# Decoding the later weights with a byte pass on ScalarE, with a longer cost table and other ranks in the planner

## The chip, the cores and the metric

The kernel runs on one core of one Trainium2 chip. The metric is the device time of one execution in microseconds. TensorE (PE) multiplies, VectorE (DVE), ScalarE (ACT) and GpSimd (POOL) do the elementwise work, and SyncE (SP) issues every DMA. Each of these engines executes its own instruction list in order.

## The reference

Four batches of attention (8 heads, 768 positions, head size 64) are followed by a mixing network. All inputs are 64-bit floats on the host; the weights reach the chip as their raw 64-bit words.

```python
scores = q @ k.T / 8 - slope[h] * dist          # only n_global = 8 first and n_local = 96 last keys kept
a = softmax(scores)                             # with + 1e-9 in the sum
x = a @ v                                       # 4 x 768 x 512
h = relu(x^T @ w_tok1) @ w_tok2                 # token mixing, 768 -> 256 -> 768
u = x + h^T
out = u + relu(u @ w_ch1) @ w_ch2               # channel mixing, 512 -> 1536 -> 512
```

## The kernel before, in words

**The work.** Attention is cut into 48 units (12 for each batch; one unit is two heads by 256 queries). A unit is a row of steps: `q` scales the queries, `S` forms scores on PE in two PSUM banks, `max` and `exp` and `norm` make the softmax on DVE, ACT and POOL, `T` and `back` transpose it (the first 20 units on PE, the later ones by DMA as `split`, `turn`, `join`), `V` multiplies by the values on PE into one PSUM bank, and `put` copies that bank out on ACT (`put` then frees it). After a batch's attention comes its token mixing (steps `N`, `J`, `U`, with `ua`, `uh`, `ul` that leave u as a high and a low part), and after it the channel mixing: 24 steps k for each batch (two halves of the positions, m = 0 and 1, by 12 slices f of the hidden layer). Step k has `F` (12 matmuls of 128x384 into one PSUM bank, tile `hp`), `fh` on ACT, `fl` on DVE (frees the bank), and `G` (12 matmuls in two halves of six, tile `acc`, four banks held through the 12 slices). All products are made of three matmuls on high and low parts.

**The weights.** They come as 30 pieces of 128x512 64-bit words: pieces 0 to 5 for the token mixing, then pairs (6 + 2f for `F`, 7 + 2f for `G`) for the 12 slices. `weights(n)` at line 281 decodes a piece into a 32-bit float: `down` (ACT) scales the upper word as a float by 2^-112 into a tile `t`, which has three buffers; `shift` (DVE) moves that left by 3; `upper` (DVE) puts in the sign bit of the upper word; `lower` (DVE) puts in the top three bits of the lower word. Then `high` (ACT) rounds to the high part and `low` (DVE or POOL, whichever the planner takes) subtracts it to get the low part, which frees `t`.

**The order.** No queue is filled in program order. Each step is registered with `add(name, engine, cost, run, after, rank, take, give)`; `Plan.record` (line 110) then plays a list schedule in which an engine that is free takes, of its ready steps whose buffers and banks are to be had, the one with the lowest rank, holds it for the cost in the table and passes on with a fixed latency. A change of the PE's kind of matmul counts 20 in rank. The order so found is written out as the order of every engine's instructions. So a cost or a rank changes the order of all engines from the moment at which the planner first decides otherwise, and the chip waits wherever its times differ from the table's.

The table holds for a piece: `down` 0.6, `shift` 0.45, `upper` 0.75, `lower` 0.85, `high` 0.52, `low` 0.64 on DVE or 1.35 on POOL. `rank` (line 736) gives weights 40 + 12n for the first six and 100 + 12n for the rest, the attention units of batch 1 120 + 8.5i, and the channel steps of batch 0 150 + 5k.

Of the kernel before, what the change touches and what calls it, by code (L numbers as in the profile page):

```python
# [9 lines left out]
F32R = mybir.dt.float32r  # L10
I32 = mybir.dt.int32
U16 = mybir.dt.uint16
I64 = mybir.dt.int64
BF16 = mybir.dt.bfloat16
AF = mybir.ActivationFunctionType
ALU = mybir.AluOpType
# [22 lines left out]
PIECES = 6 + 2 * NF  # L39

DOWN = 2.0 ** -112

HI_MIN = 2.0 ** -15


def f32(ap):
    return ap.bitcast(F32)
# [40 lines left out]
class Plan:  # L88
# [13 lines left out]
    def add(self, name, engine, cost, run, after=(), rank=0.0, take=(), give=(), form=None):  # L102

        costs = engine if isinstance(engine, dict) else {engine: cost}
        self.work[name] = dict(name=name, costs=costs, run=run, after=sorted(set(after)), rank=rank, take=take, give=give,
                               form=form, choice=isinstance(engine, dict))
# [98 lines left out]
class Fast:  # L207
# [73 lines left out]
    def weights(self, n):  # L281

        add, dve, act = self.plan.add, self.dve, self.act
        g = {}

        def load():  # L290
            x, i = self.pieces[n]
            g["w"] = self.wt.tile([P, 512], I64, tag="w", name="w64")
            self.sp.dma_start(out=g["w"], in_=x[:, i:i + 512])

        def words():
            wi = g["w"].bitcast(I32).rearrange("p (n two) -> p n two", two=2)
            return wi[:, :, 0], wi[:, :, 1]

        def down():
            g["t"] = self.io.tile([P, 512], I32, tag="io", name="t32")  # L300
            act.activation(out=f32(g["t"]), in_=f32(words()[1]), func=AF.Copy, scale=DOWN)

        def shift():
            dve.tensor_scalar(out=g["t"], in0=g["t"], scalar1=3, scalar2=None, op0=ALU.logical_shift_left)

        def upper():
            dve.scalar_tensor_tensor(out=g["t"], in0=words()[1], scalar=-0x80000000, in1=g["t"], op0=ALU.bitwise_and,
                                     op1=ALU.bitwise_or)

        def lower():  # L310
            dve.scalar_tensor_tensor(out=g["t"], in0=words()[0], scalar=29, in1=g["t"], op0=ALU.logical_shift_right,
                                     op1=ALU.bitwise_or)

        def high():
            if n < 6:
                dst, i = (self.W1, self.W2)[n // 3], 512 * (n % 3)
                g["h"], g["l"] = dst[0][:, i:i + 512], dst[1][:, i:i + 512]
            else:
                t = self.wt.tile([P, 1024], F32R, tag="w", name="wc")
                g["h"], g["l"] = t[:, :512], t[:, 512:]  # L320
                (self.A, self.Z)[n % 2][n // 2 - 3] = g["h"], g["l"]
            act.copy(out=g["h"], in_=f32(g["t"]))

        def low(engine):
            engine.tensor_tensor(out=g["l"], in0=f32(g["t"]), in1=f32(g["h"]), op=ALU.subtract)

        r = rank("weights", n)
        add(f"w{n}", "sp", 1.85, load, [f"w{n - 1}"] if n else [], rank("load weights", n), ["w", "raw"])
        add(f"down{n}", "act", 0.6, down, [f"w{n}"], r, ["t"])
        add(f"shift{n}", "dve", 0.45, shift, [f"down{n}"], r)  # L330
        add(f"upper{n}", "dve", 0.75, upper, [f"shift{n}"], r)
        add(f"lower{n}", "dve", 0.85, lower, [f"upper{n}"], r, (), ["w", "raw"])
        add(f"high{n}", "act", 0.52, high, [f"lower{n}"], r - 20, ["w"] if n >= 6 else [])
        add(f"low{n}", dict(dve=0.64, pool=1.35), 0, low, [f"high{n}"], r - 20, (), ["t"])


    def load(self, v):
# [26 lines left out]
    def pair(self, v):  # L364
# [70 lines left out]
        def halves(e, back):  # L435

            w, z = 512 - 128 * c0, 128 * c0
            by_pairs = (g["r"] if back else g["p"])[e][:, z:].bitcast(U16).rearrange("p (x two) -> p two x", two=2)
            apart = (g["p"] if back else g["r"])[e].bitcast(U16)[:, :2 * w].rearrange("p (two x) -> p two x", two=2)
            return by_pairs, apart  # L440
# [7 lines left out]
        def turned(e):  # L448
            w = 2 * (512 - 128 * c0)
            self.sp.dma_start_transpose(out=g["p"][e].bitcast(U16)[:, :w].rearrange("p (t r) -> p t r", r=P),  # L450
                                        in_=g["r"][e].bitcast(U16)[:, :w])

# [64 lines left out]
    def tokens(self, b):  # L517
# [14 lines left out]
        def split(m, c):  # L532

            g["r", m, c] = r = self.mix.tile([P, 512], F32, tag="p", name="xr").bitcast(U16)[:, :2 * HC]
            dve.tensor_copy(out=r.rearrange("p (s two x) -> p two s x", s=3, two=2),
                            in_=self.x[b, c, m].bitcast(U16).rearrange("p (s x two) -> p two s x", s=3, two=2))

# [198 lines left out]
def rank(kind, *at):  # L736

    if kind == "weights":
        return 40.0 + 12.0 * at[0] if at[0] < 6 else 100 + 12 * at[0]
    if kind == "load weights":  # L740
        n = at[0]
        return 8 + 3 * n if n < 8 else 30 + 4 * n
    if kind == "load":
        return 2.5 * at[0]
    if kind == "pair":
        v = at[0]
        b, i = divmod(v, PER)
        if b == 0:
            return 10.0 * v
        if b == 1:  # L750
            return 120 + 8.5 * i
        return BATCH * b - 60 + 8.5 * i
    if kind == "mix":
        b, k = at
        if b == 0:
            return -20.0 + k
        return (220 + 2 * k if b == 1 else BATCH * b + 10 + 3 * k)
    if kind == "channel":
        b, k = divmod(at[0], 2 * NF)
        return 150 + 5.0 * k if b == 0 else BATCH * b + 100 + 5.5 * k  # L760


BATCH = 140.0


@with_exitstack
# [5 lines left out]
def dense(ctx, tc, qT, kT, vn, nb, w1, w2, wc1, wc2, out):  # L772
# [98 lines left out]
    def decode(t, src):  # L871
        w = wk.tile([P, 768], I64, tag="dw64", name="dw64")
        n = src.shape[-1]
        nc.sync.dma_start(out=w[:, :n], in_=src)
        wi = w.bitcast(I32).rearrange("p (n two) -> p n two", two=2)[:, :n]
        lo, hi = wi[:, :, 0], wi[:, :, 1]
        ti = t.bitcast(I32)
        nc.vector.tensor_scalar(out=ti, in0=hi, scalar1=1, scalar2=1, op0=ALU.logical_shift_left,
                                op1=ALU.logical_shift_right)
        nc.vector.tensor_scalar(out=t, in0=t, scalar1=HI_MIN, scalar2=None, op0=ALU.max)  # L880
        nc.vector.tensor_scalar(out=ti, in0=ti, scalar1=3, scalar2=0x3FFFFFF8, op0=ALU.logical_shift_left,
                                op1=ALU.bitwise_and)
        nc.vector.scalar_tensor_tensor(out=ti, in0=hi, scalar=-0x40000000, in1=ti, op0=ALU.bitwise_and,
                                       op1=ALU.bitwise_or)
        nc.vector.scalar_tensor_tensor(out=ti, in0=lo, scalar=29, in1=ti, op0=ALU.logical_shift_right,
                                       op1=ALU.bitwise_or)
# [116 lines left out]
```

## Time and profile before

| | |
|---|---|
| median of 3 runs | 625.16 us (624.26 to 625.78) |
| the profiled execution | 626.12 us |
| its span, first to last instruction | 624.3 us |
| mean granted TensorE clock | 0.992 |
| PE busy | 605.2 us, 97% of the span |
| DVE busy | 369.5 us, 59% |
| ACT busy | 258.3 us, 41% |
| POOL busy | 206.2 us, 33% |

Busy times are of the one profiled execution. Matmuls are pipelined: the 12 matmuls of an `F` pass in 2.08 us while the profile gives each about 0.34 us, so PE's pace is read from starts. PEclk is the share of the full clock granted to TensorE: 1.00 is 2.4 GHz and 0.50 is 1.2 GHz. In a tile's name `wc` is a decoded weight, `w` its raw words, `sp` the bank of scores, `op` that of a unit's output, `x` the unit's output in SBUF, `o` a result on its way out.

### The profile page before, as it was taken

The numbers are of one execution on the slowest core, as the hardware profiler recorded it, in microseconds if no ns is written. First come the engines' busy times: TensorE is split into PE (matmuls) and PEld (weight loads), VectorE is DVE, ScalarE is ACT, GpSimd is POOL, SyncE is SP. The second block draws the span as 40 slices with busy tenths as digits, with TensorE's granted clock in tenths as the row PEclk, the third lists the DMA queues.
The fourth block names the chain that finished last, engine by engine and source line by source line (L and its number), as shares of the span: only waits on it lengthen the run. The fifth ranks groups of instructions, "written<-read, shape, count | busy, mean of one in ns | idle before, by whom it ended". The sixth has DMA issues, their size and how long they took to land. (4 is left out here: it accounts for less than half of the span.)

```text
span 624.3 us, 10468 instructions
## 1 busy us (share of the span) xinstructions
PE 605.2 (97%) x3730; PEld 548.0 (88%) x3730; DVE 369.5 (59%) x949; ACT 258.3 (41%) x711; POOL 206.2 (33%) x314
## 2 busy tenths in 40 slices
PE   5899998999999999999899999999999999999996
PEld 3577896998989999889788999898988999999996
DVE  4999999898733315767686437666755455113112
ACT  5899855753532102655543214444334132110110
POOL 4897755563500101534153024444131115000000
PEclk9999997999999999999999999999999999999999
DMA  7960565242550001477785101578742401001001
GB/s 258 395 225 2 203 239 200 91 148 58 120 110 1 2 0 51 64 184 156 165 163 129 38 1 51 126 145 170 168 80 47 61 1 50 1 1 52 0 1 56
DMA packets 84028, 62.63 MB, mean 100 GB/s; under 512 B 69760, under 2 KB 73984, under 8 KB 83968
## 3 DMA queue, kind: packets, MB, share of 16 engines
q1 hardware_dynamic: 83968, 61.88, 37.7%
q8 instruction: 31, 0.51, 0.3%
q14 instruction: 29, 0.24, 0.1%
HBM read 38.80 MB, written 6.29 MB: 72 GB/s over the span
## 5 line engine op out<-in xcount | busy, mean ns | idle before, releaser
L198 PE MATMUL hp<-uh,wc 128*128 128x384 f32 x768 | 211.5, 337 | 0.2 <-DVE wc L198 0.2
L198 PE MATMUL acc<-hh,wc 128*128 128x384 f32 x768 | 200.6, 342 | 0.0
L198 PEld LDWEIGHTS acc<-hh,wc 128*128 128x128 f32 x768 | 138.4, 190 | 9.3 <-issue 7.2
L198 PEld LDWEIGHTS hp<-uh,wc 128*128 128x128 f32 x768 | 140.7, 189 | 2.7 <-issue 0.9
L198 ACT ACTIVATE hh<-hp 128x384 fp32r<-128x384 f32 x96 | 47.1, 490 | 223.9 <-PE hp L198 203.5
L198 DVE SCALAR_TENSOR_TENSOR hl<-hp,hh 128x384 fp32r<-128x384 f32 x96 | 53.1, 553 | 138.6 <-ACT hh L198 138.3
L198 PE MATMUL acc<-hl,wc 128*128 128x384 f32 x384 | 129.7, 338 | 0.2 <-DVE hl L198 0.2
L198 PE MATMUL hp<-ul,wc 128*128 128x384 f32 x384 | 128.8, 336 | 0.0
L198 POOL TENSOR_SCALAR p<-p,st 128x256 f32<-128x256 f32 (+1 forms) x132 | 85.3, 663 | 58.9 <-DVE st L198 16.1
L198 DVE COPY r<-p 128x1024 uint16<-128x1024 uint16 (+1 forms) x95 | 68.9, 735 | 35.8 <-DMA p<-r 19.5
L198 ACT ACTIVATE p<-p,st 128x256 f32<-128x256 f32 (+1 forms) x132 | 63.7, 485 | 30.0 <-DVE st L198 23.1
L198 PEld LDWEIGHTS acc<-hl,wc 128*128 128x128 f32 x384 | 72.8, 190 | 0.5 <-DVE hl L198 0.5
L198 PEld LDWEIGHTS hp<-ul,wc 128*128 128x128 f32 x384 | 72.5, 189 | 0.0
L198 POOL TENSOR_TENSOR ul<-x,uh 128x384 fp32r<-128x384 f32 x24 | 24.9, 1038 | 133.3 <-ACT uh L198 85.4
L198 DVE SCALAR_TENSOR_TENSOR t<-w,t 128x512 int32<-128x512 int32 x60 | 51.8, 864 | 1.1
L198 POOL TENSOR_SCALAR qs<-e,sc 128x256 f32<-128x256 f32 x36 | 21.0, 585 | 91.4 <-DMA e<-pk 58.8
L198 PE MATMUL sp<-e,qs 64*128 64x256 f32 (+1 forms) x304 | 42.8, 397 | 5.7 <-DVE o L198 1.9
L198 PEld LDWEIGHTS sp<-e,qs 64*128 64x128 f32 x304 | 26.6, 196 | 15.9 <-issue 6.7
L198 POOL TENSOR_SCALAR pp<-pp,st 128x256 f32<-128x256 f32 (+1 forms) x60 | 34.8, 597 | 8.0 <-DVE st L198 5.7
L198 POOL TENSOR_TENSOR wc<-t,wc 128x512 fp32r<-128x512 f32 x16 | 22.6, 1415 | 19.9 <-ACT wc L198 18.6
L198 ACT ACTIVATE pp<-pp,st 128x256 f32<-128x256 f32 (+1 forms) x60 | 28.5, 485 | 1.3 <-DVE st L198 1.3
L198 PE MATMUL op<-r,e 128*64 128x128 f32 (+1 forms) x304 | 28.9, 321 | 0.0
(94 smaller groups left out, 736.6 us busy)
## 6 DMA issues: line engine op xcount, KB each, us to landing
w<-wc SPq DMA_DIRECT2D x24, 512.0 KB, 5.3
e<-pk SPq DMA_DIRECT2D x24, 512.0 KB, 3.8
out<-o SPq DMA_DIRECT2D x32, 192.0 KB, 1.9
e<-pk SPq DMA_DIRECT2D x13, 384.0 KB, 3.6
unit<-pk SPq DMA_DIRECT2D x8, 512.0 KB, 8.5
w<-w SPq DMA_DIRECT2D x6, 512.0 KB, 9.1
p<-r SPq DMA_TRANSPOSE x56, 3.2
unit<-pk SPq DMA_DIRECT2D x2, 384.0 KB, 3.8
```

The source lines that it names most:

```text
L198: ins = getattr(self.engine, name)(*args, **kw)
```

## The change

For pieces 12 to 29 the `shift` pass on DVE goes. A new ACT pass, `last`, reads byte 3 of each lower word (stride 8 bytes), scales it by 1/32 with a bias that rounds down, and writes the three bits as an integer into the lower word itself. `ends` (DVE) joins them with the sign bit in the upper word, in place; `whole` (DVE, registered under the old name `lower`) shifts `t` left by 3 and joins it with that word. Pieces 0 to 11 are decoded as before. In the table, for pieces from 6 on, `upper` or `ends` cost 0.85 in place of 0.75, `lower` or `whole` 1.3 in place of 0.85, and `low` on POOL 1.45 in place of 1.35. The ranks of the weights from piece 6 become 100 + 10n, of batch 1's units 140 + 8.5i, and of batch 0's channel steps 140 + 5k.

```diff
+U8 = mybir.dt.uint8
+BYTES = 12
+        def last():
+            w = g["w"].bitcast(U8).rearrange("p (n b) -> p n b", b=8)
+            act.activation(out=words()[0], in_=w[:, :, 3], func=AF.Copy, scale=2.0 ** -5, bias=-15.5 / 32)
+
+        def ends():
+            dve.scalar_tensor_tensor(out=words()[1], in0=words()[1], scalar=-0x80000000, in1=words()[0],
+                                     op0=ALU.bitwise_and, op1=ALU.bitwise_or)
+
+        def whole():
+            dve.scalar_tensor_tensor(out=g["t"], in0=g["t"], scalar=3, in1=words()[1], op0=ALU.logical_shift_left,
+                                     op1=ALU.bitwise_or)
...
         add(f"down{n}", "act", 0.6, down, [f"w{n}"], r, ["t"])
-        add(f"shift{n}", "dve", 0.45, shift, [f"down{n}"], r)
-        add(f"upper{n}", "dve", 0.75, upper, [f"shift{n}"], r)
-        add(f"lower{n}", "dve", 0.85, lower, [f"upper{n}"], r, (), ["w", "raw"])
+        if n >= BYTES:
+            add(f"last{n}", "act", 0.6, last, [f"w{n}"], r)
+            add(f"ends{n}", "dve", UPPER, ends, [f"last{n}", f"down{n}"], r)
+            add(f"lower{n}", "dve", LOWER, whole, [f"ends{n}"], r, (), ["w", "raw"])
+        else:
+            add(f"shift{n}", "dve", 0.45, shift, [f"down{n}"], r)
+            add(f"upper{n}", "dve", 0.75 if n < 6 else UPPER, upper, [f"shift{n}"], r)
+            add(f"lower{n}", "dve", 0.85 if n < 6 else LOWER, lower, [f"upper{n}"], r, (), ["w", "raw"])
         add(f"high{n}", "act", 0.52, high, [f"lower{n}"], r - 20, ["w"] if n >= 6 else [])
-        add(f"low{n}", dict(dve=0.64, pool=1.35), 0, low, [f"high{n}"], r - 20, (), ["t"])
+        add(f"low{n}", dict(dve=0.64, pool=1.35) if n < 6 else LOW, 0, low, [f"high{n}"], r - 20, (), ["t"])
...
-        return 40.0 + 12.0 * at[0] if at[0] < 6 else 100 + 12 * at[0]
+        return 40.0 + 12.0 * at[0] if at[0] < 6 else 100 + 10 * at[0]
...
-            return 120 + 8.5 * i
+            return 140 + 8.5 * i
...
-        return 150 + 5.0 * k if b == 0 else BATCH * b + 100 + 5.5 * k
+        return 140 + 5.0 * k if b == 0 else BATCH * b + 100 + 5.5 * k
...
+UPPER, LOWER, LOW = 0.85, 1.3, dict(dve=0.64, pool=1.45)
```

## Rows read from the trace of the kernel before

**Rows 1.** Busy by stretch: us; PE, PEld, DVE, ACT, POOL (x instructions); PEclk, DMA share, GB/s.
```profile
46.00:79.49 33.49, 33.08 (x243) 26.33 (x241) 32.89 (x100) 29.35 (x91) 26.34 (x42) 1.00 0.26 95
97.00:109.60 12.60, 10.03 (x47) 7.90 (x46) 11.72 (x30) 6.95 (x21) 7.69 (x8) 0.73 0.59 209
109.60:306.00 196.40, 196.23 (x1221) 179.61 (x1221) 118.65 (x302) 84.36 (x224) 59.70 (x85) 1.00 0.37 87
306.00:314.20 8.20, 6.31 (x33) 5.24 (x30) 5.25 (x13) 2.30 (x10) 3.15 (x6) 0.79 0.65 186
314.20:617.80 303.60, 303.40 (x1822) 286.23 (x1821) 145.33 (x339) 89.14 (x229) 67.73 (x93) 1.00 0.31 64
104.00:106.00 2.00, 2.00 (x6) 1.44 (x5) 2.00 (x12) 1.73 (x5) 1.61 (x2) 0.50 0.98 334
87.00:144.00 57.00, 54.20 (x326) 49.15 (x325) 53.05 (x109) 36.36 (x89) 32.83 (x33) 0.94 0.46 165
```

**Rows 2.** PE in order of time, 98 to 110 us: start, us, operation [idle before].
```profile
98.19 1.13 PE L198 MATMUL sp<-e,qs 64*128 64x256 f32 x8
100.40 0.67 PE L198 MATMUL sp<-e,qs 64*128 64x256 f32 x2 [1.08 <-issue]
102.56 2.07 PE L198 MATMUL sp<-e,qs 64*128 64x256 f32 x6 [1.49 <-ACT x L198]
109.83 0.52 PE L198 MATMUL acc<-hh,wc 128*128 128x384 f32 x2
```

**Rows 3.** The chain that ended last, undisturbed steps: start, us, operation.
```profile
461.94 2.30 PE hp L198 x12
465.28 2.08 PE hp L198 x12
469.44 1.06 PE sp L198 x8
```

**Rows 4.** DVE, ACT and POOL in order of time, 99 to 105 us.
```profile
99.75 0.55 DVE L198 SCALAR_TENSOR_TENSOR hl<-hp,hh 128x384 fp32r<-128x384 f32 x1
101.56 0.63 ACT L198 CAST wc<-t 128x512 fp32r<-128x512 f32 x1
101.88 2.36 DVE L198 SCALAR_TENSOR_TENSOR t<-w,t 128x512 int32<-128x512 int32 x2
102.06 0.44 ACT L198 COPY x<-op 128x128 f32<-128x128 f32 x2
102.33 1.36 POOL L198 TENSOR_TENSOR wc<-t,wc 128x512 fp32r<-128x512 f32 x1 [1.37 <-ACT wc L198]
```

**Rows 5.** PE and DVE in order of time, 305 to 315 us.
```profile
305.72 1.09 PE L198 MATMUL op<-r,e 128*64 128x256 f32 x12
307.69 0.56 DVE L198 TENSOR_TENSOR o<-acc,uh 128x384 f32<-128x384 f32 x1 [4.25 <-DMA out<-o]
308.35 0.67 PE L198 MATMUL sp<-e,qs 64*128 64x256 f32 x2 [1.54 <-DVE o L198]
314.15 0.33 PE L198 MATMUL hp<-uh,wc 128*128 128x384 f32 x1
```

**Rows 6.** DVE in order of time: the shift of piece 12; two later passes.
```profile
87.67 0.42 DVE L198 TENSOR_SCALAR t<-t 128x512 int32<-128x512 int32 x1
131.37 1.42 DVE L198 SCALAR_TENSOR_TENSOR t<-w,t 128x512 int32<-128x512 int32 x2
```

**Rows 7.** Groups of instructions by form: busy us, mean ns of one, idle before.
```profile
L198 DVE TENSOR_SCALAR t<-t 128x512 int32<-128x512 int32 x30 | 16.4, 546 | 0.0
L198 ACT ACTIVATE t<-w 128x512 f32<-128x512 f32 x30 | 20.5, 683 | 12.9 <-POOL wc L198 10.2 <-DVE wc L198 2.7
```

**Rows 8.** PE in order of time: batch 1's first and fifth scores, batch 0's first channel step.
```profile
46.14 1.01 PE L198 MATMUL sp<-e,qs 64*128 64x128 f32 x8
70.00 1.13 PE L198 MATMUL sp<-e,qs 64*128 64x256 f32 x8
79.49 0.33 PE L198 MATMUL hp<-uh,wc 128*128 128x384 f32 x1
```

## The prediction
> **What bounds the kernel now.** I read the busy times by engine first, then by stretch, then TensorE's timeline where a stretch was not full, then the other engines at those places, and the groups by form for the prices. The reader is to see in [rows 1] that PE is the bound nearly everywhere. From 109.6 to 306 us it is busy 196.23 of 196.40 us, from 314.2 to 617.8 us 303.40 of 303.60, at a granted clock of 1.00. The changed passes lie between 87 and 144 us, and most of that stretch already has PE full; a faster VectorE is worth nothing there. VectorE is nearly full as well (53.05 of 57 us), and that matters only where PE waits for it.
>
> PE's work is fixed: the change adds and takes away no matmul. So the time can only move by what PE loses in waits, in changes between kinds of matmul, and in time at the lower clock. Two places hold nearly all of the loss after 46 us.
>
> The first is at 99 to 110 us [rows 2]. The first `S` there has passed at 98.19 + 1.06 = 99.25 us (1.06 is an undisturbed `S`, [rows 3]). Up to 109.83 us, 10.58 us, PE does one more `S`, half a `G` and one `F`, which undisturbed take 1.06, 1.04 and 2.08 us, and one change of kind at 0.2 (2.30 against 2.08 in [rows 3]): 4.38 us. The loss is 6.2 us: 1.08 and 1.49 us of idle, and the rest at half clock. The granted clock is 0.50 in 104 to 106 us [rows 1], the 1.2 GHz level, after these waits, with PE working throughout; over 97 to 109.6 us it is 0.73.
>
> Why PE waited there is in [rows 4]. The second `S` needs two banks. One is freed by `fl` on DVE, which ends at 100.30 us; the matmuls begin at 100.40. The other is freed by a `put` on ACT, which begins at 102.06 and stood in ACT's order behind two rounds of decoding. ACT's `high` at 101.56 had waited for DVE's `lower`; the `put` did not need it. A round lasts some 2.75 us (the `lower` before that `high` ended about 101.5, the next ends at 101.88 + 2.36 = 104.24). The table of before gives a round's three DVE passes 0.45 + 0.75 + 0.85 = 2.05 us. So the planner believed that the `put` stood 1.4 us earlier after two rounds than it did, and the error adds up over pieces.
>
> The second place is at 306 to 314 us [rows 5]: PE finished a `V` at about 306.74 and reaches the next `F` at 314.15, 7.41 us for work of 1.06 + 0.2 + 2.08 = 3.34. The loss is 4.1 us, part of it again clock (0.79 over the stretch, [rows 1]). Here VectorE waited 4.25 us for a store to give a tile back, and the bank went late to an `S`.
>
> **The change part by part.** Removed: 18 `shift` passes, pieces 12 to 29, from 87.67 us on [rows 6]. At the group's mean of 0.546 us [rows 7] that is 9.8 us of DVE; the one in [rows 6] took 0.42, so 7.6 us is the lower end. On the path it is worth 0 by itself, since PE is full after 109.6 us and its wait before that is priced below as a place.
>
> `ends` in place of `upper`, `whole` in place of `lower`: the same form of instruction with the same count of elements, and no row shows them with all words 8 bytes apart. Free passes took 1.42 / 2 = 0.71 us [rows 6]; a blocked one 2.36 - 0.71 = 1.65 [rows 4]. I take 0.71 for `ends`, as for `upper`, and no change for `whole`. The far end is 18 x (1.65 - 0.71) = 17 us more of DVE, which would outweigh the shift; it falls in the rival on decoding below.
>
> Added: 18 `last` passes on ACT. No row shows a byte as input; `down` has the same 512 elements and stride and takes 0.683 us [rows 7], so 12.3 us; bounds 0.63 (the cast in [rows 4]) and twice 0.683. ACT is busy 36.36 of 57 us between 87 and 144 us [rows 1] and would be at 48.7: not full. `last` needs only the loaded words, so it need not wait for DVE; but if a `last` is put ahead of a late `put` or `fh`, it delays it by up to 0.68 us. PE's slack covers that after 109.6 us; I take 0. Without that cover, the bound is 12.3 us. SP's and POOL's lists get no new instruction; loads are only released earlier or later by `lower`.
>
> The table: a round is now 0.85 + 1.3 = 2.15 us planned for pieces 12 on, where I expect 0.71 + 0.71 to 1.65, and 2.6 for 6 to 11, where about 2.75 is measured. The planner will put `put`, `fl` and the decoding on ACT in an order that fits the chip better. So I take the first place as gone: -6.2 us (bounds: 0, it stays, and -6.2), and nothing for the small waits.
>
> The ranks: batch 1's units rise by 20, weights from piece 6 fall by 12 + 2(n - 6), batch 0's channel steps by 10. Five `S` of batch 1 run between 46.14 and 70.00 us [rows 8], before the first `F` at 79.49 can use any decoded piece. DVE is full there (32.89 of 33.49 us, [rows 1]); where a piece goes ahead of a unit, PE loses work that it could do at once and gains work for later only. A unit keeps PE for an `S`, a `T` and a `V`, each a little over 1 us by [rows 3, 5]: 3.1 us. I take half a unit, -6.2 + 1.5; the bounds are 0 and three units, 9.3.
>
> The second place lies 150 us behind the change, but the new order moves the store and the `S` that met there. I keep it at 0 in the sum, between -4.1 (it goes) and +4.1 (another such place arises).
>
> Sum: -6.2 + 1.5 + 0 = -4.7 us. The profiled execution took 626.12 us (span 624.3 and 1.8 around it), 1.0 us above the median of 625.16. So 621.4 by the profile's own time, and **620.5 us** as a median of runs.
>
> **The rivals.**
>
> *Both places go* and no unit is lost: 625.2 - 6.2 - 4.1 = 614.9 us. For it: each comes from one meeting of steps. Against it: an order planned anew makes its own meetings.
>
> *The decoding gets no faster and the wait stays.* In [rows 4] `lower` ends at 104.24 us, 0.55 us after POOL's `low` ends at 103.69: the `lower` pass seems held while POOL works. Then a round is `high`, `low`, `lower` in turn, 0.63 + 1.36 + 0.55 and the gaps, near 2.75 us with or without `shift`, and a `put` behind two rounds is late as now: 625.2, no change. Against it: [rows 6] has two passes at 0.71 each, so they are not always held, and the table would still order ACT better. The Trainium skill, "SBUF — State Buffer", section "SBUF: two separate sides", says that a VectorE operation with two SBUF inputs and a GpSimd operation lock a shared pair of ports against each other for a whole instruction. The trace agrees with that in the 0.55 us above; by the rule `ends`, which has two inputs as `upper` had, can be held as well, and the sum would be this rival's.
>
> *Batch 1's units go too late* (the other side). Three of the five units of [rows 8] fall behind pieces that no matmul can use before `U` is through: PE idles 3 x 3.1 = 9.3 us between 46 and 79.5 us, where it is now idle 0.4. With the first place gone that is 625.2 - 6.2 + 9.3 = 628.3. It turns the sign from two units on (6.2). For it: DVE is full there, and the ranks move by 32 and more against each other. Against it: a unit whose bank and tiles are free still goes before pieces from about 9 on, and PE's lower clock after such a wait would come on top only once.
>
> *ACT's list is held up by `last`*, so that `fh` and `put` come late after 87 us, and the second place is joined by another: 625.2 + 4.1 = 629.3.
>
> **How the numbers follow.** Chances: the forecast 0.46 (its own range 617 to 623.5), both places gone 0.14, no faster decoding 0.18, late units 0.17, ACT held up 0.05. A measurement of this kernel tells 0.2% (1.25 us) from no change. Faster: 0.46 + 0.14 + 0.02 of the third = 0.62. Same: 0.14 of the third. Slower: 0.17 + 0.05 + 0.02 = 0.24. The range leaves out most of the last rival, the upper end of late units, and the lower end of the best case: 614.5 to 628.5.
>
> **What would show it.** Right: no PE wait over 1 us between 80 and 146 us, a clock of 1.00 there, the last weights pass before 143 us, and PE's span shorter by about the 6 us of [rows 2]. Each step alone: DVE has 12 `shift` passes and ACT 18 new ones of about 0.68 us; `ends` near 0.71; the `put` ahead of an `S` not behind `high`. Wrong: idle PE between 46 and 79.5 us above 1.5 us says late units; `whole` passes ending 0.55 us after `low`, every 2.75 us, say no faster decoding. Idle PE with the clock at 0.50 after 150 us, at a store or another bank, says that the new order made its own place, which would make the prediction too low.

## The result, and the profile after

The changed kernel takes 617.4 us (616.65 to 617.69, 4 runs) against 625.47 us (624.26 to 626.06, 4 runs) for the kernel before: a ratio of 0.9865, 95% interval 0.9852 to 0.9878, or 8.1 us less. The profiled executions took 617.15 and 626.12 us. The forecast was 620.5 us, a gain of 4.7.

The head of the page of the changed kernel: busy us (share of the span) x instructions, and the granted clock in 40 slices.

```profile
span 615.2 us, 10446 instructions
PE 598.1 (97%) x3730; PEld 543.5 (88%) x3730; DVE 358.9 (58%) x923; ACT 270.6 (44%) x734; POOL 208.4 (34%) x317
PEclk9999999999999999999999999999999999999999
```

Busy times of the changed kernel in the stretches of [rows 1]; the fourth is cut 9.0 us earlier than in the kernel before, the difference of the two profiled times.

```profile
46.00:79.49 33.49, 32.49 (x243) 25.02 (x242) 30.33 (x102) 32.11 (x102) 25.52 (x42) 1.00 0.39 133
97.00:109.60 12.60, 12.60 (x90) 11.39 (x90) 11.52 (x14) 11.31 (x23) 8.79 (x6) 1.00 0.58 209
306.00:314.20 8.20, 8.20 (x53) 6.23 (x52) 4.07 (x7) 3.61 (x6) 1.35 (x1) 1.00 0.74 180
314.20:608.80 294.60, 294.60 (x1770) 279.16 (x1769) 135.37 (x329) 83.88 (x221) 59.70 (x86) 1.00 0.27 60
87.00:144.00 57.00, 56.31 (x345) 53.56 (x345) 50.08 (x67) 40.12 (x81) 33.48 (x26) 1.00 0.33 113
```

Both places that cost the kernel before its time are full now: PE works 12.60 of 12.60 us where it worked 10.03 at a clock of 0.73, and 8.20 of 8.20 us where it worked 6.31 at 0.79. PE of the changed kernel in order of time: its waits between 80 and 600 us, and the scores of batch 1 around the decoding.

```profile
72.89 1.13 PE L200 MATMUL sp<-e,qs 64*128 64x256 f32 x8
119.60 0.62 PE L200 MATMUL hp<-uh,wc 128*128 128x384 f32 x2 [0.32 <-POOL wc L200]
124.40 0.61 PE L200 MATMUL hp<-uh,wc 128*128 128x384 f32 x2 [0.36 <-POOL wc L200]
132.60 1.13 PE L200 MATMUL sp<-e,qs 64*128 64x256 f32 x8
289.09 1.14 PE L200 MATMUL sp<-e,qs 64*128 64x256 f32 x8 [1.43 <-POOL qs L200]
```

Two waits of a third of a microsecond are left where pieces are decoded, and one of 1.43 us is new at 289 us, with no loss of clock. The reader is also to see the gap: six scores of batch 1 come before the first channel step (five in [rows 8]), and then none from 72.89 to 132.60 us. In that time VectorE decodes and PE lives on `F`, `G` and what is left of earlier units. That gap belongs to this order; a faster one below does without it.

The decoding in the changed kernel, by form: `ends`, `whole` and `last`.

```profile
L200 DVE SCALAR_TENSOR_TENSOR w<-w 128x512 int32<-128x512 int32 x18 | 19.1, 1062 | 0.0
L200 DVE SCALAR_TENSOR_TENSOR t<-t,w 128x512 int32<-128x512 int32 x18 | 20.2, 1123 | 1.6
L200 ACT ACTIVATE w<-w 128x512 int32<-128x512 uint8 x18 | 11.8, 676 | 0.3 <-DMA w<-wc 0.3
```

VectorE also lost work that the byte pass did not touch: the planner now gives POOL 21 of the 24 `low` passes from piece 6 on, 16 before (the count of `wc<-t,wc` in the two profiles).

**A ledger of losses.** PE's work is the same in all these kernels, so I add up for each of ten profiled executions, in windows of 10 us from 40 to 600 us, PE's idle time and the time lost to the lower clock (the sum of 1 - PEclk times 10 us). The last column is the profiled time less both; it stays within 614 and 617 us, so the two sums leave up to 2.9 us of a difference between two kernels unexplained.

| kernel | profiled us | idle | clock | rest |
|---|---|---|---|---|
| before | 626.1 | 5.5 | 5.1 | 615.5 |
| after | 617.2 | 3.1 | 0.0 | 614.1 |
| new ranks only | 625.1 | 8.4 | 1.7 | 615.0 |
| new table only | 632.1 | 10.8 | 5.1 | 616.2 |
| byte pass only | 625.1 | 4.7 | 5.1 | 615.3 |
| table and ranks | 630.0 | 11.3 | 1.7 | 617.0 |
| byte pass and table | 626.8 | 5.8 | 5.2 | 615.8 |
| byte pass and ranks | 623.9 | 5.6 | 3.4 | 614.9 |
| new order, old decoding | 624.7 | 8.9 | 0.0 | 615.8 |
| old order, new decoding | 629.1 | 6.6 | 6.8 | 615.7 |

Between before and after the two sums differ by 7.5 us of the 9.0 by which the profiled executions differ. I worked out 10.3 us for the two places from starts where the sums give 9.6 (in both places two of the eight matmuls of an `S` have a record of 0.67 us, where all eight pass in 1.06, so the records there hide a part of the wait); 0.8 us is not assigned.

### The profile page after: what moved, and what is told of

It is laid out like the page before. It is cut to its first block, busy times and chain, and to the rows that moved or that the text cites. A ratio compares the mean times of both kernels' runs of the same rounds, so it can differ in the third digit from the quotient of the medians.

```text
span 615.2 us, 10446 instructions
## 1 busy us (share of the span) xinstructions
PE 598.1 (97%) x3730; PEld 543.5 (88%) x3730; DVE 358.9 (58%) x923; ACT 270.6 (44%) x734; POOL 208.4 (34%) x317
## 4 chain that ended last, share of the span: by engine, by line
PE 85%; POOL 2%; DMA 1%; ACT 1%; issue 1%; DVE 0%; POOLq 0%; DVEq 0%
PE acc L200 32%; PE hp L200 32%; PE pu L200 5%; PE op L200 5%; PE sp L200 5%; PE pj L200 4%; DMA e<-pk 1%; POOL wc L200 1%; PE tp L200 1%; POOL pp L200 1%; POOL p L200 0%; PE xtp L200 0%; ACT pp L200 0%; DVE o L200 0%; ACT p L200 0%
## 5 line engine op out<-in xcount | busy, mean ns | idle before, releaser
L200 PE MATMUL acc<-hh,wc 128*128 128x384 f32 x768 | 198.6, 339 | 0.0
L200 PEld LDWEIGHTS acc<-hh,wc 128*128 128x128 f32 x768 | 136.8, 188 | 8.3 <-issue 7.5
L200 POOL TENSOR_SCALAR p<-p,st 128x256 f32<-128x256 f32 (+1 forms) x132 | 76.3, 596 | 54.0 <-DVE st L200 39.6
L200 DVE COPY r<-p 128x1024 uint16<-128x1024 uint16 (+1 forms) x94 | 66.6, 719 | 26.5 <-DMA p<-r 13.3
L200 PE MATMUL sp<-e,qs 64*128 64x256 f32 (+1 forms) x304 | 39.3, 388 | 2.7 <-POOL qs L200 1.4
L200 POOL TENSOR_TENSOR wc<-t,wc 128x512 fp32r<-128x512 f32 x21 | 32.5, 1555 | 17.3 <-ACT wc L200 17.3
L200 ACT COPY x<-op 128x256 f32<-128x256 f32 (+1 forms) x64 | 18.6, 317 | 29.9 <-PE op L200 29.8
L200 DVE CUSTOM_DVE_ANT_0 p<-sp,be 128x256 f32<-128x256 f32 x48 | 20.1, 418 | 16.5 <-PE sp L200 16.5
```

The lines of the kernel that those rows point to most:

```text
L200: ins = getattr(self.engine, name)(*args, **kw)
```

## The experiments

Theory A: the order made the gain, and the lighter decoding little. Theory B: the lighter decoding made it, in whatever order. Within A, either the table or the ranks could be the part of the order that counts.

The change has three switches: the byte pass (`BYTES`), the table (`UPPER, LOWER, LOW`) and the ranks (the three lines of `rank`). All eight settings were run, which shows what each does alone and together. Off is:

```diff
-BYTES = 12
+BYTES = 30
...
-UPPER, LOWER, LOW = 0.85, 1.3, dict(dve=0.64, pool=1.45)
+UPPER, LOWER, LOW = 0.75, 0.85, dict(dve=0.64, pool=1.35)
...
-        return 40.0 + 12.0 * at[0] if at[0] < 6 else 100 + 10 * at[0]
+        return 40.0 + 12.0 * at[0] if at[0] < 6 else 100 + 12 * at[0]
...
-            return 140 + 8.5 * i
+            return 120 + 8.5 * i
...
-        return 140 + 5.0 * k if b == 0 else BATCH * b + 100 + 5.5 * k
+        return 150 + 5.0 * k if b == 0 else BATCH * b + 100 + 5.5 * k
```

| byte pass | table | ranks | median us | ratio to before (95%) |
|---|---|---|---|---|
| old | old | new | 625.03 | 0.9994 (0.9981 to 1.0007) |
| old | new | old | 631.24 | 1.0081 (1.0058 to 1.0103) |
| new | old | old | 625.64 | 0.9988 (0.9972 to 1.0005) |
| old | new | new | 631.23 | 1.0108 (1.0047 to 1.0168) |
| new | new | old | 624.80 | 0.9978 (0.9961 to 0.9996) |
| new | old | new | 623.85 | 0.9964 (0.9952 to 0.9977) |
| new | new | new | 617.4 | 0.9865 (0.9852 to 0.9878) |

No part alone makes the kernel faster, and no two give more than 0.4%. The table without the byte pass makes it slower by about 1%. Only the three together give 1.35%.

**Order apart from work.** Two kernels take the order of one and the work of the other.

The new order with the old decoding (edit to the changed kernel):

```diff
         def last():
-            w = g["w"].bitcast(U8).rearrange("p (n b) -> p n b", b=8)
-            act.activation(out=words()[0], in_=w[:, :, 3], func=AF.Copy, scale=2.0 ** -5, bias=-15.5 / 32)
+            pass
         def ends():
-            dve.scalar_tensor_tensor(out=words()[1], ...)
+            shift()
+            upper()
         def whole():
-            dve.scalar_tensor_tensor(out=g["t"], in0=g["t"], scalar=3, ...)
+            lower()
```

> The changed kernel's order, with the old decoding in it: the byte pass on ScalarE is left out, `ends` issues the old `shift` and `upper`, `whole` the old `lower`; planner, table and ranks are the changed ones. Theory A (the order made the gain): the scores of batch 1 stay out of 73 to 132 us, both waits of the kernel before stay gone, and 18 shifts of 0.42 to 0.55 us on VectorE cost little: 617 to 620 us. Theory B (the lighter decoding made it): each round gets longer by about 0.5 us, TensorE waits for pieces between 88 and 135 us, and most of the 8 us is lost: 623 to 627 us.

Measured: 624.95 us, ratio 0.9992 (0.9980 to 1.0005). The whole gain is lost though the order is the changed one. In this run: VectorE's `shift` of piece 12 and of piece 29, two waits of PE, and the busy times from 87 to 144 us.

```profile
89.17 0.41 DVE L200 TENSOR_SCALAR t<-t 128x512 int32<-128x512 int32 x1
139.41 0.41 DVE L200 TENSOR_SCALAR t<-t 128x512 int32<-128x512 int32 x1
118.59 0.62 PE L200 MATMUL hp<-uh,wc 128*128 128x384 f32 x2 [0.92 <-POOL wc L200]
124.10 0.62 PE L200 MATMUL hp<-uh,wc 128*128 128x384 f32 x2 [0.89 <-POOL wc L200]
87.00:144.00 57.00, 50.52 (x297) 45.47 (x298) 55.83 (x75) 29.60 (x59) 28.00 (x22) 1.00 0.32 112
```

The `ends` of piece 12 and of piece 29 in the changed kernel:

```profile
89.25 0.68 DVE L200 SCALAR_TENSOR_TENSOR w<-w 128x512 int32<-128x512 int32 x1
130.70 1.78 DVE L200 SCALAR_TENSOR_TENSOR w<-w 128x512 int32<-128x512 int32 x1
```

From the first of these passes to the last, 17 rounds take 41.45 us in the changed kernel, 2.44 each; with the old decoding they take 50.24 us, 2.96 each. The round grows by 0.52 us, a little more than the pass of 0.41 us that it has back, and VectorE is busy 55.83 of 57 us. Now PE waits for `F`'s pieces, seven times from 106 to 142 us, and does 50.52 us of work in the stretch where the changed kernel does 56.31. Theory B holds for this order: here the byte pass is worth the whole gain.

The old order with the new decoding (edit to the changed kernel with the old table and ranks):

```diff
-            add(f"last{n}", "act", 0.6, last, [f"w{n}"], r)
-            add(f"ends{n}", "dve", UPPER, ends, [f"last{n}", f"down{n}"], r)
-            add(f"lower{n}", "dve", LOWER, whole, [f"ends{n}"], r, (), ["w", "raw"])
...
+        add(f"down{n}", "act", 0.6, (lambda: (down(), last())) if n >= BYTES else down, [f"w{n}"], r, ["t"])
+        by = n >= BYTES
+        add(f"shift{n}", "dve", 0.45, (lambda: None) if by else shift, [f"down{n}"], r)
+        add(f"upper{n}", "dve", 0.75, ends if by else upper, [f"shift{n}"], r)
+        add(f"lower{n}", "dve", 0.85, whole if by else lower, [f"upper{n}"], r, (), ["w", "raw"])
```

> The order of the kernel before, with the new decoding in it: the old table and ranks, the place of `shift` is left empty for pieces from 12 on, the byte pass follows `down` on ScalarE, `ends` and `whole` stand where `upper` and `lower` stood. Theory A (order): the wait of TensorE at 98 to 104 us stays in the main, since the `put` stays behind the same `high`; 623 to 626 us. Theory B (lighter decoding): rounds fall from 2.75 to about 2.3 us, the `put` and `fl` come early enough, that wait and its half clock go: 617 to 620 us.

Measured: 627.30 us, ratio 1.0017 (0.9997 to 1.0036). PE, and ACT before the `put` it waits for, and the stretch from 87 to 144 us:

```profile
101.97 0.60 ACT L200 CAST wc<-t 128x512 fp32r<-128x512 f32 x1
102.47 0.41 ACT L200 COPY x<-op 128x128 f32<-128x128 f32 x2
102.94 1.65 PE L200 MATMUL sp<-e,qs 64*128 64x256 f32 x5 [2.85 <-ACT x L200]
87.00:144.00 57.00, 53.30 (x322) 48.20 (x321) 43.81 (x88) 43.84 (x102) 31.88 (x32) 0.94 0.47 168
```

VectorE is relieved (43.81 us busy against 53.05 in [rows 1]) and PE gains nothing: the `put` stands behind the same `high`, and the wait is longer than the 2.57 us in [rows 2]. The time is even above the 623 to 626 us that Theory A expected.

What that `high` stands behind can be read in both traces. First the kernel before, at the place of [rows 4]: POOL's `low`, DVE's `lower` and ACT's `down` for a later piece.

```profile
99.56 1.39 POOL L198 TENSOR_TENSOR wc<-t,wc 128x512 fp32r<-128x512 f32 x1 [1.34 <-ACT wc L198]
100.21 1.29 DVE L198 SCALAR_TENSOR_TENSOR t<-w,t 128x512 int32<-128x512 int32 x1
100.99 0.69 ACT L198 ACTIVATE t<-w 128x512 f32<-128x512 f32 x1 [0.99 <-POOL wc L198]
```

Then the same place in the old order with the new decoding: `whole`, the two `low` passes, and `down` and `last` of later pieces.

```profile
98.35 1.30 DVE L200 SCALAR_TENSOR_TENSOR t<-t,w 128x512 int32<-128x512 int32 x1
97.37 3.42 POOL L200 TENSOR_TENSOR wc<-t,wc 128x512 fp32r<-128x512 f32 x2 [1.88 <-ACT wc L200]
100.82 0.67 ACT L200 ACTIVATE t<-w 128x512 f32<-128x512 f32 x1 [0.44 <-POOL wc L200]
101.40 0.66 ACT L200 ACTIVATE w<-w 128x512 int32<-128x512 uint8 x1
```

In the kernel before two chains end together: `lower` is done at 101.50 us, and ACT is free for the `high` at 101.56, because a `down` ahead of it in ACT's list had waited 0.99 us for POOL's `low` to free one of the three `t` tiles. With the new decoding `whole` is done at 99.65 us, 1.85 us earlier, and the `high` still starts 0.41 us later, at 101.97: ACT first runs a `down` that waits for POOL until 100.82, and then a `last`. So what holds the `put` is ACT's list and POOL's `low`, and not VectorE. The `last` adds 0.57 us to this (101.40 to 101.97); without it the wait would be some 2.3 us, an estimate from these rows. Up to this place VectorE's rounds do get shorter: the five after piece 12 take 11.92 us (88.49 to 100.41) against 13.76 in the kernel before (87.67 to 101.43). Over the whole decoding they do not: 17 take 56.62 us (to 145.11) against 55.59 (to 143.26), with batch 1's units in between.

Theory A holds for this order. So neither theory was right by itself: the old order has a wait that this lighter decoding does not remove, and the new order has none only if the round is short.

**The pairs and the single parts**, in the order of the table above.

Ranks alone:

> The kernel before with the new ranks alone. By the ranks theory with old rounds of 2.75 us: pieces are wanted earlier than they come, TensorE waits for them as in the run that had the new order and the old decoding, 624 to 631 us. If ranks alone made the gain: 617 to 620 us.

Measured 625.03 us, no change, as the ranks theory expected: the second place is gone and PE waits between 80 and 140 us instead, 2.5 us for pieces, 2.3 for `fh` and `fl`, 1.0 for a `put` (8.4 us of idle in the ledger).

The table alone:

> The kernel before with the new table alone (2.6 us planned for a round, 2.75 measured). By the theory of the prediction the `put` is placed where it belongs and the first wait goes: 618 to 621 us. By the theory that rounds of 2.75 us are too slow whatever the order: a wait turns up elsewhere, 624 to 630 us.

Measured 631.24 us, above both expectations. The wait at 98 to 104 us is indeed gone, and PE waits later instead. The longest wait is for a piece (the last line below); of the 8.2 us between 80 and 165 us, 3.0 are for pieces and the rest for results of ACT and DVE (`fh`, `fl`, `join`):

```profile
97.00:109.60 12.60, 12.60 (x81) 12.53 (x79) 12.23 (x29) 9.54 (x26) 10.43 (x13) 1.00 0.62 215
109.60:150.00 40.40, 33.20 (x221) 26.52 (x220) 37.21 (x92) 32.08 (x79) 28.17 (x32) 1.00 0.70 186
137.95 0.61 PE L200 MATMUL hp<-uh,wc 128*128 128x384 f32 x2 [2.19 <-POOL wc L200]
```

The byte pass alone:

> The byte pass alone, planned with the old table (0.75 and 0.85) and the old ranks. Theory A: the planner believes a round of 1.6 us, where 2.2 to 2.5 come, so VectorE and ScalarE run behind the order as before and PE waits somewhere between 88 and 140 us: 623 to 628 us. Theory B: 617 to 620 us.

Measured 625.64 us, no change, and both places stay: Theory B, lighter work in whatever order, falls.

Table and ranks, without the byte pass:

> The new table and ranks, no byte pass (all pieces by shift, upper, lower). Theory A: the planner knows the real length of a round (2.6 planned), so the waits go; 616 to 620 us. Theory B: 623 to 627 us, with VectorE the limit as before.

Measured 631.23 us, slower than either theory expected: a table near the measured round and the new ranks do not help by themselves (11.3 us of idle; between 80 and 165 us only 2.8 are waits for pieces, and 5.0 are for results of ACT). Why this pair is worse than the ranks alone is not shown.

Byte pass and table, without the ranks:

> The changed kernel with the three old ranks: byte pass and new table. By the theory that the order needs the ranks (pieces ahead of batch 1's scores) and the byte pass only carries it: scores of batch 1 come between 80 and 130 us as before, and a wait of 1 to 3 us with half clock stays near one of them, 622 to 626 us. By the theory of the prediction (the table that fits the chip removes the wait): no such wait, 617 to 620 us.

Measured 624.80 us, within what the ranks theory expected.

Byte pass and ranks, without the table:

> The changed kernel with the old table (0.75, 0.85, 1.35): byte pass and new ranks. By the ranks theory: 617 to 620 us, with no scores of batch 1 between about 75 and 125 us. By the theory of the table: the planner believes in rounds of 1.6 us where 2.5 come, steps stand behind pieces that come late, TensorE waits several times for 0.5 to 2 us between 88 and 140 us, 622 to 627 us.

Measured 623.85 us, within what the theory of the table expected: the ranks do not carry it with the byte pass either. Its rounds are as short as the changed kernel's (41.41 us for 17), so a short round is not enough: PE waits here for `fl` (2.7 us) and for two `put`s (2.0).

In the run without the ranks PE waited for a `put` near 100 us as before; in the run without the table it waited for one near 127 us, and the clock fell after it:

```profile
100.23 1.13 PE L200 MATMUL sp<-e,qs 64*128 64x256 f32 x6 [1.26 <-ACT x L200]
```

```profile
127.62 2.07 PE L200 MATMUL sp<-e,qs 64*128 64x256 f32 x6 [1.53 <-ACT x L200]
```

All six runs with the old ranks (the kernel before, table, byte pass, byte pass with table, old order with new decoding, and the run with other stores below) have 1.7 us or more of idle PE between 300 and 320 us; none of the eight with the new ranks has more than 0.73 there. They are fewer orders than runs, since PE's order is the same in three of each: four with the old ranks, six with the new. So the second place goes with the ranks, though they touch nothing of batch 2 or later; how they remove it is not shown.

**ScalarE's share.** In the changed kernel, `down` is issued twice for pieces 12 to 29:

```diff
-            act.activation(out=f32(g["t"]), in_=f32(words()[1]), func=AF.Copy, scale=DOWN)
+            for _ in range(2 if n >= BYTES else 1):
+                act.activation(out=f32(g["t"]), in_=f32(words()[1]), func=AF.Copy, scale=DOWN)
```

> The changed kernel with `down` issued twice for pieces 12 to 29: 18 more ScalarE passes of 0.68 us, 12.3 us, unknown to the planner, the result unchanged. If ScalarE has room where the byte passes stand (36 of 57 us busy before): 617 to 619.5 us. If its list is as tight as VectorE's was: `put`, `fh` and `high` come late, TensorE waits between 88 and 140 us, 621 to 630 us.

Measured: 622.18 us (ratio to before 0.9943, 0.9926 to 0.9959): 4.8 us more than the changed kernel for 12.3 us of ScalarE that the planner does not know of. PE in this run waits for a `high` and for pieces:

```profile
122.81 0.44 PE L200 MATMUL hp<-uh,wc 128*128 128x384 f32 x1 [1.04 <-ACT wc L200]
124.17 0.61 PE L200 MATMUL hp<-uh,wc 128*128 128x384 f32 x2 [0.74 <-POOL wc L200]
```

**More pieces by bytes** (`BYTES = 6`):

> The changed kernel with the byte decoding from piece 6 on (24 pieces in place of 18). If a lighter round is what counts: two to three us of VectorE less before 88 us, 615 to 617.5 us. If the order's fit counts more: ScalarE is 92% busy between 46 and 80 us and the order changes there, a wait arises, 618 to 625 us.

Measured: 617.79 us, ratio 0.9879 (0.9848 to 0.9911), not told apart from the changed kernel. It lies just above the first expectation and below the second. The whole order is planned anew here, so the run does not price by itself what VectorE saves before 88 us.

**The measured durations in the table:**

```diff
-UPPER, LOWER, LOW = 0.85, 1.3, dict(dve=0.64, pool=1.45)
+UPPER, LOWER, LOW = 1.06, 1.12, dict(dve=0.64, pool=1.55)
```

> The changed kernel with the mean durations of its own profile in the table: `ends` 1.06, `whole` 1.12, `low` on POOL 1.55 (0.85, 1.3 and 1.45 before; their sum for a round on VectorE 2.18 against 2.15). If a truer table makes a better order: 614.5 to 618 us. If what counts is which steps happen to meet, and not the table's last tenths: another order of the same quality or worse, 617 to 624 us, with a wait in a place of its own.

Measured: 616.45 us (616.40 to 616.54), ratio 0.9852 (0.9836 to 0.9869), the lowest of all, with an interval that overlaps the changed kernel's. Its ledger has 2.9 us of idle and no clock loss, the changed kernel's 3.1: a good order need not be this one order. It does not need the gap in batch 1's scores either, nor a short round. Two `S` stand in the middle of the decoding (the third line), and 17 rounds, from `ends` of piece 12 to that of piece 29, take 56.99 us, 3.35 each, with batch 1's units in between:

```profile
86.23 0.89 DVE L200 SCALAR_TENSOR_TENSOR w<-w 128x512 int32<-128x512 int32 x1
143.22 0.68 DVE L200 SCALAR_TENSOR_TENSOR w<-w 128x512 int32<-128x512 int32 x1
116.34 2.28 PE L200 MATMUL sp<-e,qs 64*128 64x256 f32 x16
```

The run with more pieces by bytes also has three `S` between 100 and 122 us. What the fast runs share is that no step PE needs is late by much: 2.8 to 3.1 us of idle and no clock loss.

**The second wait, by other stores** (edit to the kernel before):

```diff
-            self.sp.dma_start(out=self.out[b, P * c:P * c + P, HC * m:HC * m + HC], in_=o)
+            queue = act if (b, m) == (1, 0) else self.sp
+            queue.dma_start(out=self.out[b, P * c:P * c + P, HC * m:HC * m + HC], in_=o)
```

> The kernel before with four of its 32 stores (batch 1, first half) issued from ScalarE's queue in place of SP's, at the same place in the order; all else the same. If the second wait came from stores that stood on SP behind a transpose and a load: the store leaves at about 298.5 us in place of 302.9, VectorE's wait of 4.25 us and TensorE's wait and half clock at 306 to 314 us go, the first wait stays: 621 to 622.5 us. If the bank was late for another reason: 624.5 to 627 us.

Measured: 626.01 us, ratio 1.0012 (1.0000 to 1.0023): a miss. The issue on ACT's queue and the total behind it:

```profile
301.20 0.87 ACTq L198 DMA_DIRECT2D out<-o  x2
305.44 0.56 DVE L198 TENSOR_TENSOR o<-acc,uh 128x384 f32<-128x384 f32 x1 [4.09 <-DMA out<-o]
```

The results to be stored were ready 4.9 us before the issue (at 296.32 us; in the kernel before 4.5 us, 298.40 and 302.90), since the store kept its place in the order, and on ACT it stood behind a `join` that began at 301.18. So the run did not take away what it was to take away: VectorE waits 4.09 us for the store as it waited 4.25 in [rows 5]. That the wait is one for a stored tile is shown; that SP's transposes caused it is not, and it stays open. A rival was not tested: the store itself took long. The stores of the kernel before, from issue to landing:

```profile
DMA to landing us min/median/max: 1.8/1.9/4.8
```

VectorE goes on 4.79 us after the issue at 302.90, and in the run with other stores 4.24 us after that at 301.20, each time with a load (`e<-pk`) issued within 1 us before. Had the store of the kernel before landed in the median 1.9 us, VectorE would have gone on at about 304.8, before PE was through with the `V` at 306.74: an estimate from these rows.

## Why the prediction came out as it did

The direction and the places were right. PE's work did not change; the time moved by the waits of [rows 2] and [rows 5] and the clock after them. That the sum came out near is in part luck: it gives the whole gain to the table and values the byte pass at 0, while the table alone makes the kernel slower and the changed order without the byte pass gains nothing. Point by point:

- **First place, -6.2 us: right in size, wrong in its reason.** The prediction put it down to the table, "an order that fits the chip better". The table alone does remove that wait, and PE then loses more elsewhere (631.24 us); byte pass and table together still have 1.26 us of it. In the runs made it takes all three. That the ranks keep scores, and so the `put`s they need, out of the decoding is true of the changed kernel and not the reason in general, since the fastest run has scores there. The reading behind the term was half of it: the `high` ahead of the `put` had waited for DVE's `lower` (101.50 us) and as long for a `down` that POOL's `low` held up (101.56), which the prediction did not see.
- **The byte pass, "on the path it is worth 0 by itself": wrong.** In the old order that holds (old order with new decoding: 1.0017). In the new one the round of 2.44 in place of 2.96 us is worth the whole gain, 617.4 against 624.95 us. The step took the order as given. PE was full from 109.6 us with scores of batch 1 among its work; in the changed kernel there are none from 73 to 132 us, and PE lives on the rate of decoding.
- **`ends` at 0.71 us and `last` at 0.683.** `last` took 0.676, as forecast from `down`. `ends` took 1.06 on average, held by POOL, so a round has 1.06 + 1.12 = 2.18 us on VectorE, near the table's 2.15.
- **ScalarE's 12.3 us at 0, since PE's slack covers them: not shown.** No run prices these passes. As much again costs 4.8 us where the planner does not know of it, so the slack does not cover twice as much; six more `last` passes that it did plan (more pieces by bytes) cost nothing that can be told apart.
- **Batch 1's units, +1.5 us: too much, with the wrong sign of the shift.** Six scores come before the first channel step and not fewer. PE's idle time from 46 to 79.5 us rose from 0.4 to 1.0 us, +0.6.
- **The second place, 0: this term was mis-sized most.** It went (-4.1), and a wait of 1.43 us came at 289 us: about -2.7 in sum.

With +0.6 and -2.7 the sum is -6.2 + 0.6 - 2.7 = -8.3 us. The profiled executions, from which these terms are read, moved by 9.0, the medians by 8.1. Of the rivals, "both places go" (614.9 us) came nearest in kind. "No faster decoding" is refuted for the new order by the two rounds, 2.44 and 2.96 us: taking the pass away does shorten a round, though passes are held by POOL. In the old order its outcome came true, no change: VectorE's rounds get shorter up to the first place, but the `put` comes no earlier, since POOL's `low` sets when, by way of a `down` on ACT. "Units too late" did not come about.

## What to carry to other kernels

Where a planner writes the order of all engines, a cheaper step, a truer cost and another priority are not three gains that add up: each alone left this kernel where it was or made it slower, and together they gave 1.35%. So read an edit of work off the order that it will run in: "the engine is full there anyway" holds only as long as the order that fills it stays. For a late step, read what stands ahead of it in its own engine's list, and what that waits for: here the `put` seemed to wait for VectorE, and POOL held it up just as long. And test the parts in all combinations, with the order of one and the work of the other, before one of them is called the cause.

## What the runs showed of the hardware

**The same waits with and without the lower clock.** In the run with other stores, PE met the waits of [rows 2] to within 0.02 us, and its clock stayed at 1.00 (PE's waits, and the busy times of the stretch that stands at 0.50 in [rows 1]):

```profile
100.32 0.67 PE L198 MATMUL sp<-e,qs 64*128 64x256 f32 x2 [1.10 <-issue]
102.47 1.13 PE L198 MATMUL sp<-e,qs 64*128 64x256 f32 x6 [1.48 <-ACT x L198]
104.00:106.00 2.00, 1.93 (x11) 1.61 (x10) 2.00 (x12) 1.80 (x5) 1.60 (x2) 1.00 1.01 379
```

That execution took 622.95 us. Of the 12 of this kernel, two at a mean clock of 0.999 took 622.95 and 623.21 us, and ten at 0.988 to 0.994 took 625.27 to 627.10. Only the first of the 12 has a trace; in it the waits of [rows 5] are met as well (1.72 us of idle from 300 to 320 us) and the clock stays at 1.00 there too. So the two places' waits together cost 2 to 4 us more in most executions, if the mean clock is taken as the sign, and nothing more in some, and a single profiled execution can mislead by that much.

**`ends` is held by POOL.** VectorE and POOL in the changed kernel:

```profile
105.71 1.78 DVE L200 SCALAR_TENSOR_TENSOR w<-w 128x512 int32<-128x512 int32 x1
105.22 1.73 POOL L200 TENSOR_TENSOR wc<-t,wc 128x512 fp32r<-128x512 f32 x1
```

The pass ends 0.54 us after POOL's, where a free one takes 0.68 to 0.71 us in all. The Trainium skill's rule of the shared ports ("SBUF — State Buffer", section "SBUF: two separate sides") fits this. The prediction drew from it a rival with an unchanged round; in the new order the measured rounds decide against that conclusion, not against the lock.
